# Contiguous block transposes of x, a stepped moving operand for the scores, and three orders of work in place of one

## The chip, the cores and the metric

The kernel runs on one core of one Trainium2 chip. A core has five engines with an instruction queue each: TensorE (PE, matmuls; its weight loads are shown as PEld), VectorE (DVE), ScalarE (ACT), GpSimd (POOL) and SyncE (SP, here only issuing DMA). They wait for one another by semaphores. Data lie in SBUF (128 partitions), matmul results in PSUM, inputs and outputs in the chip's DRAM. The metric is the device time of one execution in microseconds, the median over runs.

## The reference

The first part is a pair of attentions between 512 tokens and 32 states, for 8 batches and 8 heads of width 64; the second a gated feed-forward layer on its output, with a norm ahead of it.

```python
# x: (8, 8, 512, 64), state: (8, 8, 32, 64); float32
scores = x @ state^T / 8;   xread = softmax(scores)  @ state   # tokens read states
scores2 = state @ x^T / 8;  sread = softmax(scores2) @ x       # states read tokens
rows = concat([xread, sread], axis=2)  ->  (8 * 544, 512)      # heads side by side
rms = sqrt(mean(rows**2) + 1e-6)
xn = rows / rms * rms_g
out = (silu(xn @ w_gate) * (xn @ w_val)) @ w_out               # 512 -> 1536 -> 512
```

The weights arrive as float64, the output has 4352 rows of 512 float32.

## The kernel before

Heads are handled in pairs: e is the head in a pair, j the pair. The 256 state rows of all batches form a ninth, smaller batch at the end (the state stage). All matmuls are float32; each is issued as two passes, so the profile counts two matmul records for one `TE.matmul`.

**Stages.** While the weights are converted from float64, batch 0 is computed with plain products. Batches 1 to 7 follow in one loop, `for b in range(1, B)`, line 1188. In a period of this loop the feed-forward layer of batch b is computed, and beside it the attention of batch b + 1 (`tokens_read`, `states_read`) and its first weight products. Then comes the state stage.

**Feed-forward.** The first matmul (L701, `hidden_seven`) works on 2 x 2 blocks with seven products in place of eight, in six pairs of column blocks. PE writes to PSUM banks x, y, z; ACT copies them out (L747, L750, L752), DVE adds to the copies (L763), ACT applies silu (L754), DVE multiplies by the other half (L776). The weights of L701 are formed per batch by small products (L554), copied by ACT (L566) and added up by POOL (L581 to L584, `more_of_v`). The second matmul (L1003, `project_twice`) uses seven products of seven products each. Its left operands need sums of the hidden activations, which DVE forms: `quarter_sums(0)` to `quarter_sums(6)` (four instructions each, L1051, L1053, L1055, L1057) and `half_sums` (L1062). What PE has finished is copied by ACT (L1013), added to by DVE (L1043) under the names p1, p5 and u2, combined by POOL (L1029 to L1034), and stored by SP (L1111). The tiles of p1, u2 and c21 share the two buffers with the tag "g" with the copies L747 and L752 of the next stage.

**The attention of tokens.** For batches from 2 on, x lies in SBUF with 4 consecutive tokens per partition. `scores` brings it to the layout that the product needs (features on partitions) in three moves: four 32 x 32 block transposes on DVE (L316) into xB, a DMA of xB to the DRAM scratch x_d issued by ACT (L318), and four DMAs from there into xG (L323), issued by ACT as well. Then eight products of 64 x 32 tiles and 512 columns (L333), with xG as the moving operand, give the scores of the two heads of all pairs. DVE transposes them back (L342), ACT copies them (L344), and softmax steps follow (L400 to L419).

**Order of the work.** Every engine's instruction order is written out by hand. Each activity is a Python generator that issues one step and yields; a string has one letter per step, and the loop calls the generator of each letter in turn. In the loop over batches the string is `PERIOD`: h is the products of L701, t their copies on ACT, u the sums on DVE; p, c, k, o are products, copies, sums and stores of the second matmul; a and s are the two attentions of batch b + 1; v and x are weight products and their copies, w the first ones of the next batch; f, g, l are fetches. The letters q and G have a generator only for b = 1 (`weight_quarters`, `first_fetches_of_quarters`), and a letter without a generator is skipped. In the last batch, b = 7, there is no further attention; there, a stands for `others`: the steps of `state_norm` (square on ACT, sums on PE, L528 with the power on POOL, two products, then eight DVE instructions of L534 and L686) and of `sums_of_w([0])` (L658, L660, L662, L664), nine steps in all, paced by `paced`: the first falls on the twelfth a, the others on every third a from there.

Of the kernel before, what the change touches and what calls it, by code (L numbers as in the profile page):

```python
# [8 lines left out]
F32 = mybir.dt.float32  # L9
# [8 lines left out]
P = 128  # L18
# [10 lines left out]
)  # L29

PERIOD = (
    "vfhththahhtalhhuxxuttqqhufxtvqhhhtahahuuqquuutqhaquhaqttahhhhxthhuxquutxhuhuttuv"
    "kkqxxxvxhaqqhhGthhqqauuuxxqqqhkaatuGhqkuuthuaattaaahuqaqhuhuthtsusushhhuutthhGug"
    "huuqqpqtpaauufhuagpkuppkkpqsaakfgkkappcpkpakkcqkpkppapppppcqqkkkkpakppppppkppkpp"
    "pcaaaaaksssaaqaaakpppckkpppksappkskkagggcksakaakppppaooaoposkppppgkkkpasakoawssw"
    "xosspxfxlccoowxxxf"
)

STATES = (
    "hyyyyhthyytthhhuuhtuhththhytuuhuuhthuhhtthyuhyyutyhhhuuuttyuhhutyyhhthuhyhuhuttu"  # L40
    "yhuhttyuhuhuuhuthhyuthythytuhuuhuhutuuphuupcpkpcpukkcpkpkpc"
# [4 lines left out]
def kernel(  # L46
# [21 lines left out]
    VE, SE, GE, TE = nc.vector, nc.scalar, nc.gpsimd, nc.tensor  # L68

    B, H, S, D = x.shape  # L70
    Ns = state.shape[2]
    DM = H * D
    DFF = moe_w_gate.shape[1]
    NC = S // P
# [8 lines left out]
    one = ctx.enter_context(tc.tile_pool(name="one", bufs=1))  # L83
# [206 lines left out]
    def scores(b, packed, soft):  # L290

        xb = x_sb[b]
        stT = one.tile([P, 4, Ns], F32, name="stT")
        tp = aps.tile([P, 4, Ns], F32, name="at")
        TE.transpose(out=tp.rearrange("p j n -> p (j n)"),
                     in_=packed.rearrange("p e d -> p (e d)"), identity=ident)
        yield
        VE.tensor_copy(stT, tp)
        yield "step"

        if b < 2:
            xT = one.tile([P, 4, NC, P], F32, name="xT", tag="xT")
            for c in range(NC):
                tp = aps.tile([P, 4, P], F32, name="at")
                for j in range(4):
                    TE.transpose(out=tp[:, j, :], in_=xb[:, c, P * j:P * j + P], identity=ident)
                yield
                SE.copy(xT[:, :, c, :], tp)
                yield "step"
            xT = xT.rearrange("p j c t -> p j (c t)")  # L310
        else:


            xB = one.tile([P, 4, 4, Ns, NC], F32, name="xB", tag="xT")
            for q in range(4):
                VE.transpose(out=xB[:, q].rearrange("p j t c -> p j c t"), in_=xb[:, q // 2::2, :, Ns * (q % 2):Ns * (q % 2) + Ns])  # L316
                yield
            nc.scalar.dma_start(out=x_d[b % 2].rearrange("q g f r -> (g f) q r"),  # L318
                                in_=xB.rearrange("p q j t c -> p q (j t c)"))
            yield  # L320
            xT = one.tile([P, 4, 4, P], F32, name="xG", tag="xT")
            for q in range(4):
                nc.scalar.dma_start(  # L323
                    out=xT[Ns * q:Ns * q + Ns].rearrange("f g j r -> f g (j r)"),
                    in_=x_d[b % 2][q].rearrange("g f r -> f g r"))
                yield
            xT = xT.rearrange("p g j r -> p j g r")


        sp = [aps.tile([P, S], F32, name="at") for e in range(2)]  # L330
        for j in range(4):
            for e in range(2):
                TE.matmul(out=sp[e][Ns * j:Ns * j + Ns, :], lhsT=stT[D * e:D * e + D, j, :],  # L333
                          rhs=xT[D * e:D * e + D, j],
                          start=True, stop=True)
        yield


        sS = read[b] = (one if b else x_0).tile([P, 2, NC, P], F32, name="sS")
        eS = one.tile([P, 2, S // Ns, Ns], F32, name="eS", tag="eS")  # L340
        for e in range(2):
            VE.transpose(out=eS[:, e].rearrange("p k n -> p (k n)"), in_=sp[e])  # L342
            yield
            SE.copy(sS[:, e].rearrange("p c t -> p (c t)"), sp[e])  # L344
            yield "step" if e else None

        soft.update(st=stT, e=eS)
# [168 lines left out]
    def state_norm():  # L516

        sq = one.tile([P, NI, NT], F32, name="sqT", tag="eS")
        SE.activation(out=sq, in_=xsT, func=ACTF.Square, scale=DM ** -0.5)
        yield  # L520
        sp = aps.tile([P, NT // P], F32, name="at")
        for r in range(NT // P):
            for i in range(NI):
                TE.matmul(out=sp[:, r:r + 1], lhsT=sq[:, i, P * r:P * r + P], rhs=ones,
                          start=(i == 0), stop=(i == NI - 1))
        yield
        ss = two.tile([P, NT // P], F32, name="sst")
        VE.tensor_scalar(ss, sp, 1e-6, None, op0=ALU.add)  # L528
        ri = mean_root(ss, NT // P)
        yield  # L530
        rp = along_rows(ri, NT // P)
        yield
        for i in range(NI):
            VE.scalar_tensor_tensor(out=xsT[:, i, :], in0=xsT[:, i, :], scalar=rms_g[:, i:i + 1],  # L534
                                    in1=rp[:, 0:NT], op0=ALU.mult, op1=ALU.mult)
        sums_of_x()
        yield
# [113 lines left out]
    def sums_of_w(mps):  # L651

        for mp in mps:
            a11, a12, a21, a22 = blocks_of_w(mp)
            s12 = seven["v"].tile([P, 2, HI, 2, P], F32, name="v")
            s4 = seven["vs"].tile([P, 3, 2, P], F32, name="vs")[:, 0:HI]
            w_sums[mp] = s12[:, 0], s12[:, 1], s4
            VE.tensor_tensor(out=s12[:, 0], in0=a21, in1=a22, op=ALU.add)  # L658
            yield
            VE.tensor_tensor(out=s12[:, 1], in0=s12[:, 0], in1=a11, op=ALU.subtract)  # L660
            yield
            VE.tensor_tensor(out=s4, in0=a12, in1=s12[:, 1], op=ALU.subtract)  # L662
            yield
            VE.tensor_tensor(out=a21, in0=a11, in1=a21, op=ALU.subtract)  # L664
            yield
# [423 lines left out]
    def fetches_of_quarters(b):  # L1089

        for n in range(7 * (b - 1) + 3, 7 * b + 3):
            fetch_quarters(n)
            yield
# [26 lines left out]
    done = object()  # L1120
# [28 lines left out]
        for part in own:  # L1149
            yield from part[0]  # L1150

    def paced(steps):

        yield from range(11)
        while True:
            if next(steps, done) is done:
                break
            yield from range(3)
        while True:
            yield  # L1160

    parts_0, banks_0 = {}, []
    load_state(0)
    load_x(0, nc.scalar, nc.sync)
# [15 lines left out]
    with tc.manual_schedule(**by_hand):  # L1180
        for stream in ORDER:
            if stream in "ckw" and "s" not in seven:
                early.close()
                open_late()
            next(streams[stream])
        assert all(next(stream, done) is done for name, stream in streams.items() if name != "z")

        for b in range(1, B):
            h, t, u = hidden_seven(S, weights_of(b), lambda b=b: tokens_of(b), True)
            p, c, k, o = project_twice(b, store_tokens(b))  # L1190
            own = [own_weights(b, mp) for mp in range(2, NM // 2)]
            then = [own_weights(b + 1, mp) for mp in range(2)] if b + 1 < B else []
            others = None
            streams = {"h": h, "t": t, "u": u, "p": p, "c": c, "k": k,
                       "v": (step for part in own for step in part[0]),
                       "x": (step for part in own + then for step in part[1])}
            streams.update(o=o, f=fetches(b), g=fetches_of_quarters(b))
            if b == 1:
                streams.update(q=weight_quarters(), G=first_fetches_of_quarters())
            if b + 1 < B:  # L1200
                streams.update(l=loads(b + 2) if b + 2 < B else iter((0, 0)), a=tokens_read(b + 1), s=states_read(b + 1),
                               w=first_products(b + 1, then))
            else:
                others = paced(step for part in (state_norm(), sums_of_w([0])) for step in part)
                streams["a"] = others
            for stream in PERIOD:
                if stream in streams:
                    step = next(streams[stream], done)
                    assert step is not done or b + 1 == B
            assert all(next(stream, done) is done for stream in streams.values() if stream is not others)  # L1210
        n = B * (NM // 2)
        h, t, u = hidden_seven(NT, (state_weights, state_sums), state_tokens, True,
                               lambda mp: fetch(n + mp + W_BUFS))
        p, c, k = project_seven(NT, store_states, nc.scalar)
        list(weights_back())
        streams = {"h": h, "t": t, "u": u, "p": p, "c": c, "k": k, "y": sums_of_w(range(1, NM // 2))}
        for stream in STATES:
            next(streams[stream])
        assert all(next(stream, done) is done for stream in streams.values())
# [29 lines left out]
```

## Time and profile before

| | |
|---|---|
| Median of 3 runs | 772.78 us (772.61 to 774.09) |
| The profiled execution: time | 772.66 us |
| The profiled execution: span of its instructions | 770.5 us |
| PE busy | 750.9 us, 97% of the span |
| PE weight loads busy | 594.9 us, 77% |
| DVE busy | 618.1 us, 80% |
| ACT busy | 354.4 us, 46% |
| POOL busy | 296.2 us, 38% |
| Granted TensorE clock | full throughout |
| DMA | 146.15 MB, mean 190 GB/s |

Times inside the profile are microseconds from the start of the span. A row of the timeline has the start, the length, the engine, the line, the operation, the tile written and the tiles read, the shape and how often; in brackets stands how long the engine had been idle before it, and what ended that wait. A row of one line's instructions has the count, and the shortest, the median and the longest duration in nanoseconds. A row of stretches gives the window, its length, and the busy time and the number of instructions of PE, PEld, DVE, ACT and POOL, then the granted clock, the DMA share and GB/s. The chain of waits is followed back from the last instruction: at each step to what released it, or to the one before it on its engine. PE's ends are modelled: a row of matmuls is longer than the distance to the next one's start.

### The profile page before, as it was taken

How to read it: one execution, taken by the hardware profiler on the slowest of the kernel's cores; microseconds unless marked ns; L12 is line 12 of the kernel's file. 1: busy time of each engine (PE TensorE's matmuls, PEld its weight loads, DVE VectorE, ACT ScalarE, POOL GpSimd, SP SyncE). 2: the span in 40 equal slices, each digit the busy share in tenths (PEclk: the TensorE clock that was granted, in tenths of full speed). 3: DMA queues.
4: the chain of work that ended last, by engine and by line, in shares of the span. 5: the costliest groups of instructions: out<-in, count | busy, mean ns of one | idle time of the engine just before them, and what ended most of it. 6: DMA issues, size and time to landing. Idle time of an engine off the chain costs nothing.

```text
span 770.5 us, 14346 instructions
## 1 busy us (share of the span) xinstructions
PE 750.9 (97%) x5608; PEld 594.9 (77%) x5608; DVE 618.1 (80%) x1000; ACT 354.4 (46%) x548; POOL 296.2 (38%) x379
## 2 busy tenths in 40 slices
PE   6999999999999999999999999999999999999998
PEld 5643445778877898879977997889878988899996
DVE  4999988679957997689957995799579974799561
ACT  5798875454235523554165424552355236511220
POOL 2100003884585225642375039402852256324400
PEclk9999999999999999999999999999999999999999
DMA  9877844855786266825684367616862665052311
GB/s 292 252 255 245 312 179 130 320 173 199 255 260 236 55 231 224 310 58 198 188 306 130 127 202 256 237 43 234 255 236 53 233 199 223 1 200 75 124 55 27
DMA packets 61890, 146.15 MB, mean 190 GB/s; under 512 B 15744, under 2 KB 32640, under 8 KB 54912
## 3 DMA queue, kind: packets, MB, share of 16 engines
q1 hardware_dynamic: 48704, 125.78, 47.7%
q10 hardware_dynamic: 13120, 19.47, 8.8%
q8 instruction: 44, 0.72, 0.4%
q14 instruction: 22, 0.18, 0.1%
HBM read 116.46 MB, written 28.77 MB: 188 GB/s over the span
## 4 chain that ended last, share of the span: by engine, by line
PE 67%; DVE 27%; issue 3%; ACT 1%; POOL 1%; DMA 0%; SPq 0%; DVEq 0%; POOLq 0%
PE f L701 31%; PE f L1003 12%; PE f L803 5%; PE pv L597 5%; DVE hb L1062 4%; PE at L554 3%; PE pv L554 3%; DVE hb L776 3%; PE f L866 2%; DVE h L1057 2%; DVE h L1051 2%; DVE h L1053 2%; DVE g L763 1%; DVE hs L782 1%; DVE kept L1043 1%
## 5 line engine op out<-in xcount | busy, mean ns | idle before, releaser
L701 PE MATMUL f<-aT_s,v 128*128 128x256 f32 x504 | 117.7, 381 | 0.0
L701 PEld LDWEIGHTS f<-aT_s,v 128*128 128x128 f32 x504 | 94.7, 190 | 19.2 <-ACT v L566 5.9
L763 DVE TENSOR_TENSOR g<-g,f 128x512 f32<-128x512 f32 (+1 forms) x96 | 61.2, 648 | 51.1 <-PE f L701 31.0
L1029 POOL TENSOR_TENSOR kept<-kept 128x256 f32<-128x256 f32 x28 | 23.4, 838 | 202.8 <-DVE z L414 113.3
L701 PE MATMUL f<-aT_t,vs 128*128 128x256 f32 x336 | 87.5, 384 | 0.5 <-DVE g L763 0.4
L1003 PE MATMUL f<-w,h 128*128 128x128 f32 x588 | 75.4, 278 | 4.3 <-DVE h L1053 4.3
L754 ACT ACTIVATE hb<-g 128x1024 f32<-128x1024 f32 (+1 forms) x48 | 48.2, 1005 | 67.6 <-DVE g L763 67.6
L701 PEld LDWEIGHTS f<-aT_t,vs 128*128 128x128 f32 x336 | 62.2, 190 | 18.1 <-issue 6.9
L1003 PEld LDWEIGHTS f<-w,h 128*128 128x128 f32 x588 | 69.8, 192 | 6.7 <-DVE h L1053 5.8
L1013 ACT COPY kept<-f 128x512 f32<-128x512 f32 (+1 forms) x56 | 28.8, 540 | 73.2 <-PE f L1003 68.9
L566 ACT COPY v<-pv 128x512 f32<-128x512 f32 x42 | 22.6, 592 | 79.5 <-PE pv L554 78.1
L277 POOL TENSOR_TENSOR ri<-ss,mhalf 128x4 f32<-128x4 f32 x8 | 11.3, 1407 | 118.8 <-DVE ss L357 116.2
L581 POOL TENSOR_TENSOR vs<-v 128x256 f32<-128x256 f32 x42 | 31.3, 744 | 61.7 <-ACT v L566 61.7
L701 PE MATMUL f<-aT_t,v 128*128 128x256 f32 x168 | 44.4, 387 | 1.6 <-DVE c L763 1.5
L803 PE MATMUL f<-wo,hb 128*128 128x512 f32 x96 | 44.7, 598 | 0.0
L752 ACT COPY g<-f 128x512 f32<-128x512 f32 (+1 forms) x48 | 26.9, 561 | 38.1 <-PE f L701 38.1
L597 PE MATMUL pv<-aT_s,v 128*128 128x512 f32 x96 | 44.2, 597 | 0.0
L701 PE MATMUL f<-aT_s,vs 128*128 128x256 f32 x168 | 43.8, 383 | 0.0
L776 DVE TENSOR_TENSOR hb<-hb,c 128x512 f32<-128x512 f32 (+1 forms) x48 | 39.2, 816 | 5.0 <-ACT hb L754 4.8
L1003 PE MATMUL f<-wo,h 128*128 128x128 f32 x336 | 42.3, 275 | 0.0
L1003 PE MATMUL f<-wo,hb 128*128 128x128 f32 x336 | 42.1, 275 | 0.0
L1003 PEld LDWEIGHTS f<-wo,hb 128*128 128x128 f32 x336 | 40.3, 192 | 0.4
(179 smaller groups left out, 1704.9 us busy)
## 6 DMA issues: line engine op xcount, KB each, us to landing
w_m<-w_d SPq DMA_DIRECT2D x48, 1024.0 KB, 6.6
w<-t_d SPq DMA_DIRECT2D x49, 576.0 KB, 4.1
out_dram<-kept SPq DMA_DIRECT2D x56, 128.0 KB, 3.4
raw<-in_moe_w_val_dram SPq DMA_DIRECT2D x6, 1024.0 KB, 5.2
raw<-in_moe_w_out_dram SPq DMA_DIRECT2D x6, 1024.0 KB, 7.5
w_d<-w_m SPq DMA_DIRECT2D x6, 1024.0 KB, 4.9
x_b<-in_x_dram SPq DMA_DIRECT2D x6, 1024.0 KB, 7.6
x_d<-xB ACTq DMA_DIRECT2D x6, 1024.0 KB, 4.2
```

The source lines that it names most:

```text
L554: TE.matmul(out=pv[e][Ns * j:Ns * j + Ns, :], lhsT=stT_g[b][D * e:D * e + D, j, :], rhs=w[D * e:D * e + D, j].rearrange("p m k f -> p (m k ...
L581: GE.tensor_tensor(out=vs[:, 0], in0=a21, in1=a22, op=ALU.add)
L597: TE.matmul(out=to[0], lhsT=lhs(i, k), rhs=r, start=(i == 0), stop=(i == len(rhs) - 1))
L701: TE.matmul(out=ps[:, i, 0:half], lhsT=l[:, i, :], rhs=r, start=(start and i == 0 and k == 0), stop=(k == len(lhs) - 1), skip_group_check= ...
L752: SE.copy(gates(q)[1], q["x"][:, :, 0:half])
L754: SE.activation(out=hb[:, 2 * mp:2 * mp + 2, 0:n].rearrange("p m (c t) -> p m c t", c=2), in_=q["g"][:, :, :, 0:half], func=ACTF.Silu if s ...
L763: VE.tensor_tensor(out=to, in0=to, in1=q[ps][:, :, 0:half], op=ALU.add)
L776: VE.tensor_tensor(out=part, in0=part, in1=val, op=ALU.mult)
L803: TE.matmul(out=banks[r], lhsT=hb[:, m, P * r:P * r + P], rhs=wo[:, m, :], start=(m == 0), stop=(m == NM - 1))
L1003: TE.matmul(out=to[half][:, slot, :], lhsT=lhs[:, k, :], rhs=rhs[:, k, :], start=(fresh and n in (0, 4) and k == 0), stop=(k == QM - 1), s ...
L1013: SE.copy(k[:, 4 * i:4 * i + 4 - i], banks[name][i])
L1062: VE.tensor_tensor(out=to[:, k:k + QM], in0=a[:, k:k + QM], in1=b[:, k:k + QM], op=ALU.subtract)
```

## The change

Three things change together.

- The block transposes write xB as [partition, q, j, c, t] in place of [partition, q, j, t, c]. The rows that one instruction writes are contiguous; before, neighbours were 4 floats apart. Here t is a token's partition within a group of 32 and c its place among the 4 tokens of a partition.
- x_d and xG get the same inner order, with DMAs of the same sizes. The products of the scores read xG through a view with the axes g, t, c, whose innermost step is 32 floats. The result has its tokens in the order that it had before.
- The string is split: `FIRST` (b = 1) is the old `PERIOD`, `PERIOD` (b = 2 to 6) the old one without q and G, which had no generator there, and `LAST` (b = 7) lists the last batch's steps with no skipping and without `paced`. With the letters that did nothing taken out, the old string and `LAST` have all steps in the same order but for those of a: the first two of the nine stay, the other seven come later.

```diff
 PERIOD = (
+    "vfhththahhtalhhuxxutthufxtvhhhtahahuuuuuthauhattahhhhxthhuxuutxhuhuttuvkkxxxvxha"
+    "hhthhauuuxxhkaatuhkuuthuaattaaahuahuhuthtsusushhhuutthhughuuptpaauufhuagpkuppkkp"
+    "saakfgkkappcpkpakkckpkppapppppckkkkpakppppppkppkpppcaaaaaksssaaaaakpppckkpppksap"
+    "pkskkagggcksakaakppppaooaoposkppppgkkkpasakoawsswxosspxfxlccoowxxxf"
+)
+
+FIRST = (
     "vfhththahhtalhhuxxuttqqhufxtvqhhhtahahuuqquuutqhaquhaqttahhhhxthhuxquutxhuhuttuv"
...
 )
-
+LAST = (
+    "vfhththhhthhuxxutthufxtvhhhthhuuuuuthuhtthhhhxthhuxuutxhuhuttuvkkxxxvxhhhthhuuux"
+    "xhktuhkuuthuattahuhuhuthtuuhhhuutthhughuuptpuufhuagpkuppkkpkfgkkppcpkpakkckpkppp"
+    "ppppckkkkpkppppppkppkpppcakaakpppckkpppkppkkkgggckakkppppooopokppppgkkkpakoopcco"
+    "o"
+)
...
-            xB = one.tile([P, 4, 4, Ns, NC], F32, name="xB", tag="xT")
+            xB = one.tile([P, 4, 4, NC, Ns], F32, name="xB", tag="xT")
             for q in range(4):
-                VE.transpose(out=xB[:, q].rearrange("p j t c -> p j c t"), in_=xb[:, q // 2::2, :, Ns * (q % 2):Ns * (q % 2) + Ns])
+                VE.transpose(out=xB[:, q], in_=xb[:, q // 2::2, :, Ns * (q % 2):Ns * (q % 2) + Ns])
                 yield
             nc.scalar.dma_start(out=x_d[b % 2].rearrange("q g f r -> (g f) q r"),
-                                in_=xB.rearrange("p q j t c -> p q (j t c)"))
+                                in_=xB.rearrange("p q j c t -> p q (j c t)"))
...
-            xT = xT.rearrange("p g j r -> p j g r")
+            xT = xT.rearrange("p g j (c t) -> p j g t c", c=NC)
...
-    def paced(steps):
-
-        yield from range(11)
-        while True:
-            if next(steps, done) is done:
-                break
-            yield from range(3)
-        while True:
-            yield
...
-            others = None
...
             else:
-                others = paced(step for part in (state_norm(), sums_of_w([0])) for step in part)
-                streams["a"] = others
-            for stream in PERIOD:
-                if stream in streams:
-                    step = next(streams[stream], done)
-                    assert step is not done or b + 1 == B
-            assert all(next(stream, done) is done for stream in streams.values() if stream is not others)
+                streams["a"] = (step for part in (state_norm(), sums_of_w([0])) for step in part)
+            for stream in FIRST if b == 1 else LAST if b + 1 == B else PERIOD:
+                next(streams[stream])
+            assert all(next(stream, done) is done for stream in streams.values())
```

More of the change, by code (lines that the diff above doesn't have):

```diff
@@ L36 @@
     "xosspxfxlccoowxxxf"
+)
+LAST = (
+    "vfhththhhthhuxxutthufxtvhhhthhuuuuuthuhtthhhhxthhuxuutxhuhuttuvkkxxxvxhhhthhuuux"
+    "xhktuhkuuthuattahuhuhuthtuuhhhuutthhughuuptpuufhuagpkuppkkpkfgkkppcpkpakkckpkppp"
+    "ppppckkkkpkppppppkppkpppcakaakpppckkpppkppkkkgggckkakppppooopokppppgkkkpakoopcco"
+    "o"
 )
```

## The prediction

> **What bounds the kernel now.** I read the page first, then the stretches between equal points of successive batches, then the chain of waits in order of time, then rows of the timeline around the changed steps.
>
> ```profile
> PE 750.9 (97%) x5608; PEld 594.9 (77%) x5608; DVE 618.1 (80%) x1000; ACT 354.4 (46%) x548; POOL 296.2 (38%) x379
> ```
>
> PE is the bound on average. Cut at the start of each batch's L496 products, the middle of the kernel is a period of about 81.7 us (us, then the busy time of each engine):
>
> ```profile
> 221.04:302.74 81.70, 81.30 (x667) 68.14 (x670) 67.05 (x115) 35.62 (x58) 35.24 (x46) 1.00 0.58 194
> 302.74:384.41 81.67, 81.13 (x666) 68.03 (x670) 66.85 (x115) 35.63 (x58) 35.19 (x46) 1.00 0.58 194
> 630.02:712.86 82.84, 81.69 (x665) 71.43 (x664) 63.27 (x97) 30.60 (x50) 39.01 (x51) 1.00 0.37 128
> ```
>
> PE shows some 0.5 us of idleness in a period. But "busy" counts the tail of a matmul. Start to start, undisturbed 128x256 records stand 0.216 us apart and 128x128 records 0.112 us; what is beyond that sums to 2.5 to 3.3 us in a period. Some 2 us of it are steps of about 0.1 us that recur at the same places. So at most about 1.1 us of a period is PE really waiting. The chain says where:
>
> ```profile
> 249.35 2.80 PE f L701 x12
> 252.15 0.02 issue
> 252.18 0.70 DVE g L763
> ...
> 282.62 1.14 DVE eS L417
> 283.77 0.48 DVE h L1053
> 284.25 0.04 issue
> 284.29 4.29 PE f L1003 x36
> ```
>
> From 252 to 284 DVE holds the chain, before and after it PE does. Now where the changed instructions lie, seen on DVE in the next batch:
>
> ```profile
> 321.17 1.18 DVE L316 STREAM_TRANSPOSE xB<-x_b 128x512 f32<-128x512 f32 x1
> 322.12 0.74 DVE L776 TENSOR_TENSOR hb<-hb,c 128x512 f32<-128x512 f32 x1
> 322.73 1.13 DVE L316 STREAM_TRANSPOSE xB<-x_b 128x512 f32<-128x512 f32 x1
> 323.64 0.73 DVE L776 TENSOR_TENSOR hb<-hb,f 128x512 f32<-128x512 f32 x1
> 325.41 1.29 DVE L763 TENSOR_TENSOR g<-g,f 128x512 f32<-128x512 f32 x2 [1.04 <-ACT g L752]
> ...
> 333.07 1.48 DVE L763 TENSOR_TENSOR g<-g,f 128x512 f32<-128x512 f32 x2 [2.00 <-PE f L701]
> ...
> 340.14 1.30 DVE L342 STREAM_TRANSPOSE eS<-at 128x512 f32<-128x512 f32 x2
> ```
>
> The transposes are over by 323.9, and at 333.07 DVE has waited 2.00 us for PE. This wait is the anchor of my argument: the stretch that DVE sets starts only there.
>
> [...] DVE transposes that write f32 at a step of 16 bytes (L316) take 1142 ns, those with contiguous rows (L342) 701 ns; and ACT's exponentials, L459, which for batches from 2 on write at a step of 128 bytes, show the same:
>
> ```profile
> L316 DVE STREAM_TRANSPOSE xB<-x_b x24: 1105/1142/1201, 144.1 to 568.1; 128x512 f32<-128x512 f32 x24
> L459 ACT ACTIVATE e<-sS,s x16: 705/1203/1244, 77.5 to 609.6; 128x512 f32<-128x512 f32 x16
> ```
>
> No run here shows a PE read with a step. [...] L333's eight products of a pass, 64x32 tiles, start 0.007 us apart and run together.
>
> **The change part by part.**
>
> Transposes. Four in each of six batches. Followed by another instruction, a stepped one holds DVE for about 0.95 us (321.17 to 322.12), a contiguous one for 0.60. That frees 4 x 0.35 = 1.4 us of DVE per batch, 8.4 us in all. Value on the path: about nothing, since it all lies ahead of the anchor, where DVE idles already (1.04 us at 325.41, 2.00 at 333.07); the bubbles of PE near 321 to 331 are only the recurring 0.1 us. The write to x_d then leaves ACT up to 1 us earlier (ACT's copy of v waits 1.4 us per batch behind it), but the reads into xG are issued some 7 us later, behind copies of v that wait for PE, so they do not move. Their sizes do not change. Bounds: 0 to -0.2 us per batch; I take 0.
>
> Scores' products. Eight per batch, each two passes over 512 columns; the moving operand now steps by 32 f32 (128 bytes) between neighbours. Undisturbed they take 1.05 us from their start to the next product's:
>
> ```profile
> 338.07 1.11 PE L333 MATMUL at<-xG,stT 64*32 64x512 f32 x16
> 339.12 1.13 PE L701 MATMUL f<-aT_s,vs 128*128 128x256 f32 x4
> ...
> 583.48 1.90 PE L333 MATMUL at<-xG,stT 64*32 64x512 f32 x16
> 585.32 1.13 PE L701 MATMUL f<-aT_s,vs 128*128 128x256 f32 x4
> ```
>
> The trace contains an experiment on delay here: in two batches (at 419.75 and 583.48) the products waited inside for xG and took 1.72 and 1.84 us, and yet those periods were 81.77 and 81.88 us against 81.67 for the batch at 338; their sum of PE gaps was 2.5 us against 3.1. So 0.7 us of delay is paid for by PE waits that were there. Why: L342 on DVE starts at 340.14, when its scores have been done since about 339.2; PE then catches up in gaps of 0.6 us some 5 us later and 0.56 us at L1003. The free slack is so about 0.95 us; more delays DVE and is paid in full.
>
> The cost of the stepped read is not in the trace. From below: a read that costs no more than now, since PE takes one f32 in 0.84 ns (429 ns for 512) [...]. In the middle: the writes' price, 0.95 us less some 0.07 fixed over 512, 1.7 ns per element, against 0.84: each pass 0.9 us instead of 0.43, +0.95 us per batch. From above: [...] a pass some three times as long or more, +2.1 us per batch. I take something up to +0.7, hidden; the lower half of this interval. With +0.4, the batch at 583.48 has 0.79 + 0.4 - 0.95 = 0.2 us over its slack, that at 419.75 0.1, the others none: +0.3 us. Batch 2 (168.46) has DVE at 172.04, 2 us of slack.
>
> Order of the last batch (FIRST repeats the old string and PERIOD is the old one less letters that did nothing, so nothing else moves). The state norm and the first sums of w, nine steps, come later. Step 5 (L534 and L686, eight DVE instructions, 683.65 to 686.9, about 3.1 us) moves from inside quarter_sums(2), behind its L1051, to just before quarter_sums(4); L658 and L660 (0.65 us each) follow behind the L1051 of that, L662 goes ahead of quarter_sums(6), and L664 between the two L1043 of the last sum u2. No instruction and no wait is added, and no DMA is moved; step 3's small DVE and POOL work and step 4's two products move by a few instructions, covered by DVE's running work. Two PE waits stand in this region:
>
> ```profile
> 693.69 1.60 PE L1003 MATMUL f<-w,h 128*128 128x128 f32 x12 [0.79 <-DVE h L1053]
> ...
> 712.86 1.16 PE L701 MATMUL f<-x_t,v 128*128 128x128 f32 x8 [0.36 <-ACT g L747]
> ```
>
> The first, 0.96 us by starts, goes: the L1053 of quarter_sums(3) is done by about 690.8 instead of 693.6, and PE wants it at 692.7. Gain 0.86. But the second, 0.53 us by starts, follows from u2: L1043 at 705.46, POOL's sums from 706.26, two stores issued at 710.15 and 710.53, landed near 712.35, then ACT's L747 into that buffer. Behind the moved work DVE reaches quarter_sums(6) at about the old time (702.0), and u2's additions at about 705.0 to 707.0 with L664 (0.65 to 1.2 us) between them, so POOL's second sum still starts near 707.1. What PE gained it waits here, about 1.4 us in place of 0.53. Net 0, with bounds -0.9 and +0.7.
>
> Sum: 772.66 us is the profiled execution (span 770.5 and 2.16 around it); transposes 0, products +0.3, last batch 0; it lies 0.12 below the median of 772.78. So 772.78 + 0.3 = 773.1 us.
>
> **The rivals.**
>
> B, the read costs what the writes cost. [...] Against it: these are writes. Overrun of the slack: at 256.38 (1.24 us before) 0.2, at 419.75 0.67, at 501.80 0.05, at 583.48 0.8: +1.7 us, 774.5.
>
> C, slower by the reads of several streams from the same partitions. Against it: the contiguous products run eight at a time at full rate. +2.1 us per batch overruns by 1.3, 1.2, 1.8, 1.2, 2.0 and in batch 2 by 0.4: +7.9, 780.7 us. It decides from some 1.3 us added per batch on.
>
> D, faster: both waits of the last batch vanish (0.86 + 0.43) and earlier transposes give back 0.07 us of gaps in each batch, 0.4: -1.7, 771.1. For it: DVE is lighter in the last batch until 694. Against: u2's path through POOL and the stores.
>
> That it doesn't do what it says: a stepped source in the transposes (runs of 128 bytes, unchanged) might hold them above 0.70 us; the time would be the same, as they are hidden.
>
> **How the numbers follow.** A (hidden) 0.40, B 0.22, C 0.20, D 0.18. A change of 0.2% is 1.55 us, about what a measurement of this kernel can tell from none: faster is below 771.2, slower above 774.3. D is faster: 0.18. A and nearly half of B are the same: 0.50. The rest of B and C are slower: 0.32. A's own range is 772.2 to 774.0. The range takes in A, B, most of D and the lighter half of C: 770.9 to 779.5, leaving about 0.15 outside.
>
> **What would show it.** The L316 row near 0.70 us; DVE's wait ahead of L763 at the anchor longer by about what was freed there (2.0 to 3 us), and the start of L342 unmoved in its period. The L333 rows: 1.05 to 1.7 us for A, 2.0 for B, 3 or more for C, with the start of L342 behind them then. In the last batch the wait for L1053 gone and that for L747 longer. Wrong it would be if periods fell by over 0.3 us with the transposes, or if the first L701 products of the state stage no longer waited for L747.

## The result and the profile after

The changed kernel takes 775.92 us (median of 6 runs, 775.09 to 776.80), the kernel before 773.30 us beside it (6 runs, 772.61 to 774.73). The ratio is 1.0033, with a 95% interval of 1.0020 to 1.0046: slower by about 2.6 us.

The profiled execution took 776.58 us, the second slowest of the six, for a span of 774.5. Of its 4.0 us over the span before, 1.5 lie ahead of batch 1, where nothing was changed. That stretch lasts from 128.1 to 129.6 us in the profiles here, and both lengths occur with the old layout and with the new one, so this part is not put down to the change.

The changed lines first (one line's instructions: count, shortest, median and longest duration in ns). L328 is the old L316, L345 the old L333; the first row is the old L333 before, the other two are after.

```profile
L333 PE MATMUL at<-xG,stT x96: 586/589/613, 168.5 to 584.8; 64*32 64x512 f32 x96
L328 DVE STREAM_TRANSPOSE xB<-x_b x24: 668/703/712, 145.5 to 571.3; 128x512 f32<-128x512 f32 x24
L345 PE MATMUL at<-xG,stT x96: 1031/1043/1126, 169.7 to 588.2; 64*32 64x512 f32 x96
```

By medians, the transposes went from 1142 to 703 ns, and the scores' matmul records from 589 to 1043. The periods of batches 2 to 6, cut at the same points as before (now L508), in the view by stretches: first the three before that are not shown above, then all five after.

```profile
384.41:466.18 81.77, 81.38 (x667) 68.30 (x670) 66.91 (x115) 35.64 (x58) 35.37 (x46) 1.00 0.59 194
466.18:548.14 81.96, 81.42 (x666) 68.00 (x670) 67.04 (x115) 35.63 (x58) 35.17 (x46) 1.00 0.57 193
548.14:630.02 81.88, 81.49 (x667) 68.33 (x670) 67.00 (x115) 35.63 (x58) 35.30 (x46) 1.00 0.58 193
222.08:304.28 82.20, 81.81 (x664) 68.39 (x663) 66.55 (x115) 35.74 (x58) 34.83 (x46) 1.00 0.57 193
304.28:386.24 81.96, 81.57 (x663) 68.24 (x662) 66.22 (x115) 35.76 (x58) 34.87 (x46) 1.00 0.57 193
386.24:468.32 82.08, 81.69 (x663) 68.35 (x662) 66.33 (x115) 35.75 (x58) 34.88 (x46) 1.00 0.58 193
468.32:551.56 83.24, 82.58 (x664) 68.33 (x663) 66.34 (x115) 35.77 (x58) 34.88 (x46) 1.00 0.57 190
551.56:633.79 82.23, 81.83 (x664) 68.41 (x663) 66.41 (x115) 35.75 (x58) 34.77 (x46) 1.00 0.57 192
```

DVE's busy time fell by some 0.6 us in a period, PE's rose, and each period is longer: 82.20, 81.96, 82.08, 83.24 and 82.23 against 81.70, 81.67, 81.77, 81.96 and 81.88, together 2.7 us. Batch 1's stretch is 0.35 us shorter, and what follows the last of these points is longer by only 0.1 us (140.66 against 140.56 from the first product of L508 or L496). So the loss lies in the five middle periods.

The timeline of PE and DVE around the products of one batch, to be set against the row at 338.07 before:

```profile
334.68 1.48 DVE L775 TENSOR_TENSOR g<-g,f 128x512 f32<-128x512 f32 x2 [2.00 <-PE f L713]
...
339.68 2.00 PE L345 MATMUL at<-xG,stT 64*32 64x512 f32 x16
341.61 1.13 PE L713 MATMUL f<-aT_s,vs 128*128 128x256 f32 x4
...
341.75 1.31 DVE L354 STREAM_TRANSPOSE eS<-at 128x512 f32<-128x512 f32 x2
```

The products last 1.93 us from their start to the next one's, 1.05 before. DVE's wait ahead of the anchor is still 2.00 us: the time that the transposes freed is already lost ahead of it. And DVE reaches L354 without a wait here, though the period is 0.3 us longer.

### The profile page after: what moved, and what is told of

Same layout as the page of the kernel before. It is cut to its first block, busy times and chain, and to the rows that moved or that the text cites. A ratio compares the mean times of both kernels' runs of the same rounds, so it can differ in the third digit from the quotient of the medians.

```text
span 774.5 us, 14346 instructions
## 1 busy us (share of the span) xinstructions
PE 755.8 (98%) x5608; PEld 596.9 (77%) x5608; DVE 613.4 (79%) x1000; ACT 355.1 (46%) x548; POOL 294.9 (38%) x379
## 4 chain that ended last, share of the span: by engine, by line
PE 76%; DVE 17%; POOL 2%; issue 2%; DMA 1%; ACT 1%; SPq 0%; DVEq 0%; ACTq 0%; POOLq 0%
PE f L713 35%; PE f L1015 14%; PE f L815 5%; PE pv L609 5%; PE at L566 3%; DVE hb L1074 3%; PE pv L566 2%; PE f L1147 2%; PE f L878 2%; PE at L345 2%; DVE h L1063 2%; DVE h L1069 1%; DVE h L1065 1%; DVE hb L788 1%; DVE kept L1055 1%
## 5 line engine op out<-in xcount | busy, mean ns | idle before, releaser
L1015 PE MATMUL f<-w,h 128*128 128x128 f32 x588 | 75.3, 278 | 3.5 <-DVE h L1065 3.5
L1015 PEld LDWEIGHTS f<-w,h 128*128 128x128 f32 x588 | 69.8, 192 | 5.7 <-DVE h L1065 4.8
L788 DVE TENSOR_TENSOR hb<-hb,f 128x512 f32<-128x512 f32 (+1 forms) x48 | 31.1, 649 | 15.7 <-PE f L713 15.3
L788 DVE TENSOR_TENSOR hb<-hb,c 128x512 f32<-128x512 f32 (+1 forms) x48 | 40.8, 850 | 3.5 <-ACT hb L766 3.3
L713 PEld LDWEIGHTS f<-aT_s,vs 128*128 128x128 f32 x168 | 30.8, 190 | 14.7 <-issue 8.7
L1015 PE MATMUL f<-wo,h 128*128 128x128 f32 x336 | 42.1, 275 | 0.0
```

What stands on the lines that cost most here:

```text
L713: TE.matmul(out=ps[:, i, 0:half], lhsT=l[:, i, :], rhs=r, start=(start and i == 0 and k == 0), stop=(k == len(lhs) - 1), skip_group_check= ...
L788: VE.tensor_tensor(out=part, in0=part, in1=val, op=ALU.mult)
L1015: TE.matmul(out=to[half][:, slot, :], lhsT=lhs[:, k, :], rhs=rhs[:, k, :], start=(fresh and n in (0, 4) and k == 0), stop=(k == QM - 1), s ...
```

## The experiments

**The two halves of the change.** The first kernel takes the data side alone, the second the strings alone.

```diff
 # first: before, with
-VE.transpose(out=xB[:, q].rearrange("p j t c -> p j c t"), in_=...)
+VE.transpose(out=xB[:, q], in_=...)            # xB as [p, q, j, c, t]; so its DMA
-xT = xT.rearrange("p g j r -> p j g r")
+xT = xT.rearrange("p g j (c t) -> p j g t c", c=NC)
 # second: before, with FIRST, PERIOD and LAST as in the change
```

> The data side of the change alone (contiguous transposes, stepped moving operand), with the old string and its paced letters. Theory R (the stepped read lengthens the scores' products from 1.05 to about 2 us per batch, PE waits of 0.6 us cover a part, nothing else matters): about 2.5 us slower than before, the products' records near 1.04 us in place of 0.60. Rival O (the new order of the last batch costs the time): as before, within 0.5 us. Rival T (the earlier transposes and the earlier write to x_d disturb the transfers): slower too, but with scores' products that wait for xG by more than before.

> The three strings alone, on the old data layout. R: as before within 0.5 us; in the last batch the wait at the second matmul's fourth product goes and comes back at the first products of the state stage (the profile after shows 1.7 us there against 0.5). O: about 2.5 us slower. If the order gains what it removes: 0.9 us faster.

Measured: the data side 776.64 us, ratio 1.0035 (1.0023 to 1.0048); the strings 773.46 us, ratio 1.0008 (0.9999 to 1.0016), both against 773.04. The loss belongs to the data side. The strings do nothing that the measurement resolves, and their profile shows what they do: of the two PE waits in the last batch the first is gone, and the second, at the first products of the state stage, has grown by starts from 0.53 to 1.69 us. In the changed kernel the same rows of the timeline read:

```profile
716.36 0.37 ACT L759 COPY g<-f 128x256 f32<-128x256 f32 x1 [2.36 <-POOL kept L1043]
...
716.78 1.16 PE L713 MATMUL f<-x_t,v 128*128 128x128 f32 x8 [1.51 <-ACT g L759]
```

**Which part of the data side.** Both kernels are the changed one with another view of xG for the products; the tokens of batches 2 to 7 then come out in another order, and the amount of work is the same.

```diff
-xT = xT.rearrange("p g j (c t) -> p j g t c", c=NC)         # step of 32 floats
+xT = xT.rearrange("p g j (h two) -> p j g two h", two=2)    # third: step of 2 floats
+xT = xT.rearrange("p g j r -> p j g r")                     # fourth: contiguous
```

> The changed kernel, but the moving operand is read with a step of 2 floats (8 bytes) in place of 32; this puts the tokens of batches 2 to 7 in another order, the work is the same. [...] the products' records at 0.60 us, the eight products in 1.05 us, the time as before within 0.5 us. If any step costs: records of 1.04 us and about 2.6 us slower than before.

> The changed kernel with the moving operand read contiguously, so that the tokens of batches 2 to 7 come out in another order; the contiguous transposes and the new strings stay. R: as before within 0.5 us, because the 1.4 us of DVE freed per batch lie ahead of a wait of 2 us. If the freed DVE time is worth something: 2 to 8 us faster than before. Rival T: still slower than before by 1 us or more.

Measured: 773.30 us with a step of 8 bytes, ratio 0.9999 (0.9990 to 1.0007); 772.71 us with the contiguous read, ratio 0.9995 (0.9987 to 1.0004). The fourth kernel keeps the fast transposes (702 ns) and the strings, and is as fast as before: the transposes bring nothing that the measurement resolves. The third keeps a step, and has no loss:

```profile
L345 PE MATMUL at<-xG,stT x96: 606/612/655, 169.4 to 585.8; 64*32 64x512 f32 x96
```

(The view of one line's instructions in the third kernel: a median of 612 ns, where the contiguous read before has 589 and the changed kernel 1043.)

**The delay by itself, and the smallest step that costs.** The fifth kernel is the one before with the products of batches 2 to 7 issued twice, contiguous as they were. The sixth is the changed one with a step of 4 floats, tokens in another order again.

```diff
-for j in range(4):                            # fifth, in scores
+for j in [*range(4)] * (2 if b > 1 else 1):
-xT = xT.rearrange("p g j (c t) -> p j g t c", c=NC)         # sixth
+xT = xT.rearrange("p g j (h two) -> p j g two h", two=4)
```

> The kernel before, but for batches 2 to 7 the eight contiguous products of the scores are issued twice in a row, so that they take about 2.0 us in place of 1.05 with no stepped read at all. If the stepped read acts only through its length: 2 to 3 us slower than before, with periods of 82.0 to 82.5 us, as the change. If it also hinders other readers of the memory: less slow than the change by 1 us or more. If up to 0.95 us per batch were hidden, as predicted: at most 1 us slower.

> The changed kernel with a step of 4 floats (16 bytes) in the moving read, tokens of batches 2 to 7 in another order. [...] records of 1.04 us, eight products in 1.9 us or more, 2.6 us slower than before, as with the step of 128 bytes. If the price grows with the distance: records between 0.60 and 1.04 us.

Measured: issued twice 776.55 us, ratio 1.0040 (1.0026 to 1.0053); a step of 16 bytes 776.38 us, ratio 1.0039 (1.0024 to 1.0054). Contiguous products of about the same total length cost what the stepped ones cost, so the stepped read acts through its length, and no harm to other readers is needed to explain the loss. In the sixth, the records take 1075 ns, against 1043 with the step of 128 bytes: 16 bytes cost as much as 128. One batch's products of the fifth, and the line of the sixth:

```profile
338.69 2.70 PE L333 MATMUL at<-xG,stT 64*32 64x512 f32 x32
...
L345 PE MATMUL at<-xG,stT x96: 1056/1075/1112, 169.7 to 589.6; 64*32 64x512 f32 x96
```

**What covers a part of it.** The seventh and the eighth kernel move the last two DVE instructions of `quarter_sums(0)` from behind DVE's wait at the anchor to ahead of it, in all three strings; the seventh has the old layout, the eighth the stepped read.

```diff
-"...uttuvkkxxxvxhahhthhauuuxxhkaatuhkuuth..."     # PERIOD; FIRST and LAST alike
+"...uttuvkkkkxxxvxhahhthhauuuxxhaatuhuuth..."
```

> The new strings on the old data layout, with the last two instructions of quarter_sums(0) (two DVE instructions per batch) moved from behind DVE's wait of 2 us to before it. If the 0.6 us that hide a longer scores product are DVE's load behind that wait: the PE gaps some 40 us into each period go, periods of 81.1 to 81.8 us by how late xG lands, and 1 to 3 us faster than before. If that slack comes from elsewhere: as before within 0.5 us.

> The changed kernel with the same two DVE instructions moved. If DVE's load was the cover: with the cover gone the stepped read is paid in full, 0.9 us in each of five or six periods, so 4 to 5.5 us slower than the run with the old layout and the same move. If the cover is independent of DVE: 2.5 us slower than that run, as in the change.

Measured: 771.53 us with the old layout, ratio 0.9973 (0.9962 to 0.9983), and 776.25 us with the stepped read, ratio 1.0035 (1.0022 to 1.0047), both against 773.55. The same data side costs 2.6 us in the kernel as it was and 776.25 - 771.53 = 4.7 us when DVE carries less behind the anchor. So DVE's load there is what covered a part of it. The seventh's own profile does not show the gain in the middle periods: it is of the slowest of its eight runs, 773.03 us, xG landed late in it (products of 1.15 to 1.75 us in batches 3 to 7), and its five periods sum to 408.9 us as before (409.0).

**When xG lands.** In many profiles the products are longer than either 1.05 or 1.93 us, because they wait inside for the last piece of xG. The ninth kernel is the changed one with its four reads into xG issued ahead of ACT's copies of v, in the strings of batches 1 to 6. The tenth has the strings and the old layout with this and with the move of the seventh.

```diff
-"...uttuvkkxxxvxhahhthhauuuxxhkaatuhkuuth..."     # PERIOD
+"...uttuvkkaaaaxxxvxhhhthhuuuxxhktuhkuuth..."     # ninth
+"...uttuvkkkkaaaaxxxvxhhhthhuuuxxhtuhuuth..."     # tenth
```

> The changed kernel with the four reads into xG issued some 2.5 us earlier on ACT in batches 1 to 6, so that they have landed when the products start. If the change's loss is 1.93 us of products against a cover of 0.6 and the rest waiting for xG inside the products: all products of batches 3 to 7 at 1.93 us, periods of 81.97 us, 1.3 to 1.8 us slower than before. If xG's lateness plays no part: 2.6 us slower.

> The new strings on the old layout, with the two DVE instructions moved as in the seventh experiment and the reads into xG issued earlier. If the lateness of xG took part of that move's gain: products of 1.05 us, periods of 81.1 to 81.2 us, 2.5 to 3.5 us faster than before. If not: 2 us faster, as there.

Measured: the ninth 774.90 us, ratio 1.0029 (1.0017 to 1.0041); the tenth 768.88 us, ratio 0.9951 (0.9938 to 0.9964), both against 773.12. In the profile of the ninth all products of batches 3 to 7 last 1.93 to 1.95 us and the five periods 81.98 to 82.00, as expected; but the times do not separate it from the change itself. The tenth is faster than both kernels, by 4.2 us against the one before. Four of its five middle periods (the first, 81.76 us, has a further PE wait of 0.6 us):

```profile
301.81:382.88 81.07, 80.68 (x667) 68.20 (x670) 66.84 (x115) 35.62 (x58) 35.77 (x46) 1.00 0.59 195
382.88:463.95 81.07, 80.67 (x667) 68.20 (x670) 66.95 (x115) 35.62 (x58) 35.88 (x46) 1.00 0.59 195
463.95:545.06 81.11, 80.72 (x667) 68.09 (x670) 66.82 (x115) 35.63 (x58) 35.72 (x46) 1.00 0.58 195
545.06:626.13 81.07, 80.67 (x667) 68.17 (x670) 66.71 (x115) 35.63 (x58) 35.85 (x46) 1.00 0.58 195
```

PE's share of them is the same as ever, and they are 0.6 us shorter: these 0.6 us are what DVE's load had cost in a period before.

**Contiguous everywhere.** The eleventh kernel is the tenth with contiguous transposes, the contiguous read and contiguous exponentials; the tokens stay in the order c, t up to the stores, which put them back. The twelfth leaves the stores and the exponentials as they were, so that the tokens of batches 2 to 7 come out in another order.

```diff
+to = rows_[P * r:P * r + P]                   # eleventh, in store_tokens
+if b > 1:
+    to = to.rearrange("(t c) n -> c t n", c=NC)
-nc.sync.dma_start(out=rows_[P * r:P * r + P], in_=ot)
+nc.sync.dma_start(out=to, in_=ot)
```

> A version meant to be faster than both: contiguous transposes and a contiguous moving read, tokens kept in the order c, t within each 128 through the feed-forward layer and put back by the stores (rows 4 apart, 32 per group), ACT's exponentials contiguous, the two DVE instructions moved and xG read earlier. If transposes and exponentials are hidden: as the tenth experiment within 0.5 us. If the freed DVE and ACT time counts once the cover is thin: 0.5 us or more faster than that. If the stores suffer from their order: slower than that.

> The tenth kernel (two DVE instructions moved, xG read earlier) with contiguous transposes and the contiguous read, stores as before, so that the tokens of batches 2 to 7 come out in another order. It separates the transposes from the stores of the eleventh. If the transposes are hidden even with a thin cover: as the tenth within 0.5 us, 768.4 to 769.4. If the 1.4 us of DVE per batch now count: 0.5 us or more faster than the tenth.

Measured: the eleventh 796.49 us, ratio 1.0301 (1.0287 to 1.0316) against 773.12; the twelfth 768.33 us, ratio 0.9936 (0.9922 to 0.9949) against 773.25. The eleventh loses over 23 us by its stores. From its costliest groups (busy us, mean ns, idle before and what ended it):

```profile
L759 ACT COPY g<-f 128x512 f32<-128x512 f32 (+1 forms) x48 | 26.8, 557 | 37.3 <-DMA out_dram<-kept 25.3
```

ACT waits 25.3 us for stores out of buffers that it wants to write, and PE waits 18.8 us in all for this copy (1.5 in the tenth). Six of PE's waits last 2.3 to 4.1 us. In each of them or within 1.5 us after it the granted clock falls to 0.50, in five cases for 3.4 us and in one for 6.8, 23.9 us together (the mean over the span of 794.7 us is 0.985); no other profile here has such a stretch before its last 2 us (means of 0.999 to 1.000). At half the clock PE loses about half of that time, an estimate of 12 us, so the slow clock is a good part of the loss beside the waits themselves. A pair of stores of the last batch, with nothing beside it, moves at some 90 GB/s for about 3 us; in the tenth kernel at up to 344 GB/s for 1.3 us. The mean busy share of the 16 DMA engines in these 3 us is 0.2, against 0.6 to 0.9 in the tenth. What it is in this order of the rows that slows the stores was not shown; other forms of the store were not tried. The twelfth is 0.55 us below the tenth by medians from different series, with overlapping intervals. Their profiles tell more: the twelfth's five middle periods last 81.06 or 81.07 us, and the tenth's undisturbed ones the same, so the transposes do not count there even with the thin cover.

## Why the prediction was right or wrong

The time, 775.92 us, lies in the range of 770.9 to 779.5, which was drawn to take in the rivals too, and outside the likeliest case's own, 772.2 to 774.0. The likeliest case was A, a cost that is hidden. What came was slower, and its mechanism is rival B's; B's own figure, 774.5, was too low because it used the same slack as A.

**The transposes**: right. 703 ns, and nothing gained by it (fourth kernel). One detail was not as said: the wait at the anchor should have grown, and is 2.00 us as before, since DVE waits earlier, too (1.11 us at 326.56, for PE), and the freed time is lost before it gets to the anchor.

**The stepped read**: the first term that failed. I took "something up to +0.7, hidden; the lower half of this interval" for a batch; it was +0.88. The value in the middle, worked out from the stepped writes of DVE (0.9 us for a pass, products of 2.0 us), was the right one: they last 1.93 us. (The fixed 0.07 us in it is an estimate from the trace before, where DVE's 128x384 instructions start 0.47 us apart and its 128x512 ones 0.60.) I held against it that those were writes; the runs show that reads by PE pay about as much: 0.96 us for a pass of 512, half of 1.93, where a stepped transpose of 512 held DVE for 0.95. Rival C, a price for several streams from the same partitions, fell; its +2.1 us was my assumption, which no trace showed.

**The slack**: the second term that failed. I put it at 0.95 us, from the start of L342 and from two PE waits, 0.6 and 0.56 us, that should shrink. Only the first did. PE before and after, from 4.6 us (5.5 us after) behind the start of the products:

```profile
342.68 1.03 PE L701 MATMUL f<-aT_t,vs 128*128 128x256 f32 x4
343.86 1.13 PE L701 MATMUL f<-aT_t,v 128*128 128x256 f32 x4 [0.15 <-DVE c L763]
344.91 1.10 PE L701 MATMUL f<-aT_t,vs 128*128 128x256 f32 x4
345.85 1.03 PE L701 MATMUL f<-aT_s,vs 128*128 128x256 f32 x4
...
345.17 1.03 PE L713 MATMUL f<-aT_t,vs 128*128 128x256 f32 x4
346.03 1.03 PE L713 MATMUL f<-aT_t,v 128*128 128x256 f32 x4
346.89 1.03 PE L713 MATMUL f<-aT_t,vs 128*128 128x256 f32 x4
347.76 1.03 PE L713 MATMUL f<-aT_s,vs 128*128 128x256 f32 x4
```

The same three steps take 3.17 us before, where PE waits for DVE's sums, and 2.59 after: 0.58 us are given back here. The wait at L1003 (L1015 after) stands at 0.55 to 0.57 us in every kernel's middle periods, with the products at 1.02 or at 2.7 us. It is no reserve: probably it belongs to a loop from PE through DVE's `half_sums` and `quarter_sums(3)` back to PE, which moves along when PE is late; this was not tested. The profiles of before, after and the first six experiments follow one line: with products of length L a period takes 81.69 us up to L = 1.66, and 81.69 + L - 1.66 beyond (L = 1.93: 81.96 measured; 2.38 in the first experiment: 82.43; 2.72: 82.77). The exception is one period of the five in each of them (two in the sixth), longer by 0.3 to 0.8 us: PE is held up there, some 15 us from the period's start, in most cases by a copy that itself waits for a store. So 1.66 - 1.04 = 0.62 us are covered. That DVE's load behind the anchor is this cover, the seventh, eighth and tenth kernels show: with two instructions taken out from behind it, the flat part of the line is gone and the slope goes on below 1.66 (1.60 in the seventh: 81.64; 1.02 in the tenth: 81.07).

With the two terms at their measured size my own sum gives the loss: delays before of 0.19, 0, 0.67, 0.06 and 0.79 us, each plus 0.88 less 0.62, make 0.45, 0.26, 0.93, 0.32 and 1.05, 3.0 us, of which the kernel before already paid 0.05 and 0.17: 2.8, and 2.6 was measured.

**That xG lands late** in some batches was seen, but as a fixed delay of two of them. It differs from profile to profile (1.02 to 1.83 us of contiguous products in batches 3 to 7), and the tenth kernel's early reads remove it.

**The last batch**: right. 0.96 us gone at one wait, 1.2 us more at the other, for the reason given: u2's additions, POOL's sums, two stores, then ACT's copy into their buffer. (The profile names POOL as the releaser; in the trace before, ACT's wait for the second store ended at 712.35, and the copy began at 712.43.) The strings alone give 1.0008, with 1 inside the interval. So rival D, that both waits vanish, fell.

## What to carry to other kernels

Here, time freed ahead of a wait for another engine was worth nothing until some work was moved into it: what moved two instructions across that wait brought 2.0 us, where transposes faster by 0.44 us each brought none. Before a gap is counted as a reserve, it should be asked whether it shrinks when the engine comes late: a delay that the trace already contains shows it by the sum of gaps, and one has to look which of them shrank. Steps of 16 and of 128 bytes were not free for the matrix engine either (1075 and 1043 ns a record, 589 contiguous); moving one from a hidden DVE write into a PE read that was only partly covered was a bad trade here, even for 0.9 us.

## What the runs showed of the hardware

- A float32 moving operand of TensorE, 512 columns, 64 x 32 tiles, eight at a time: contiguous 589 ns a record (median), a step of 8 bytes 612, of 16 bytes 1075, of 128 bytes 1043. I had not expected that the price is there in full at 16 bytes and no higher at 128.
- All eight products of a pass still run side by side with the step: 16 records in 1.93 us, the first eight of them started within 0.05 us, against 1.02 us without.
- A pair of stores of 128 rows of 1 KB, in a view with 4 as its first axis, moved at some 90 GB/s for about 3 us, a pair with plain rows at up to 344 GB/s for 1.3 us, and the kernel with such stores lost 3%.
- In that kernel (mean granted clock 0.985), and in no other profile here before its last 2 us (means of 0.999 to 1.000), the granted clock stood at 0.50 for a while: five stretches of 3.4 us and one of 6.8, each with a PE wait of 2.3 to 4.1 us during it or less than 1.5 us before it. PE's waits of up to 1.5 us, in all the profiles, had none: at the changed kernel's of 1.51 us, at 716.78, the clock was 1.00.
